# Query loads four slots sooner, and a new order of the last pair's products, in a fused attention and MLP kernel

## The chip, the cores and the metric

The kernel runs on one core of one Trainium2 chip. The metric is the device time of one execution in microseconds (us). Six runs of the kernel before have a median of 292.06 us (291.69 to 293.18).

## The reference

There are 8 batches of 8 heads, 576 positions and 64 features, in float32. Each batch goes through a linear attention with a cosine weighting, and its result through a two-layer network with a squared ReLU:

```python
q_p, k_p = phi(q), phi(k)      # phi(x) = [relu(x)*cos, relu(x)*sin], 128 features
kv  = einsum('bhsf,bhsd->bhfd', k_p, v);  z = sum(k_p, axis=2)
num = einsum('bhsf,bhfd->bhsd', q_p, kv)
den = einsum('bhsf,bhf->bhs', q_p, z)[..., None] + 1e-06
x   = (num / den) laid out as 4608 tokens x 512
h   = x @ w_in                 # 512 -> 2048
out = (relu(h) ** 2) @ w_out   # 2048 -> 512
```

## The kernel before

**Tiles and stages.** A batch is 576 tokens: four blocks of 128 (the "main" part) and a tail of 64. The tails of two neighbouring batches are handled together. `gemm1` makes h for 256 tokens (or for a double tail) in slices, ScalarE applies the ReLU into `rt`, VectorE squares it into `gT`. `gemm2` multiplies `gT` with `w_out`; from batch 1 on it does so for pairs of 128-token blocks with a seven-product scheme of the Strassen kind (`pair_mm`). A pair has two row blocks and two column halves of 256, so four result blocks `y[:, row, half]`. Seven products of eight 128x128x256 matmuls each (`product`, L523) go into four accumulators: `ya` and `yc` from the PSUM pool with the tag "yps", `yv` and `yu` from the pool with the tag "hps", which the h tiles of `gemm1` also use. VectorE forms sums of the left operand (`g_sum`, tiles `gs`, called S(1) to S(4)) and combines the products with `add` (L537). ScalarE copies two products out (`s1` at L561, `s5` at L576).

**The order of the work.** Nothing is scheduled automatically. A list of 144 slots holds one slice of `gemm1` or `gemm2` each; for every batch its `gemm1` slots start at `first[b]` and its `gemm2` slots at `second[b]`. For batches 2 to 7 `first` is 34, 50, 72, 88, 106, 122, and `second` is 42, 60, 80, 98, 114, 132. `at(slot, function, ...)` hangs further work behind a slot, `late` hangs the `g_sum` calls there, and `run` emits slot after slot. Each engine then works off its own instructions strictly in that order; engines wait for one another by semaphores alone. Attention work of a later batch is thus woven between the matmuls of an earlier one.

**Around the moved load.** For batches 4 to 7 the loop at L686 plans the attention of batch b while `gemm2` of batch b-2 runs. With o = second[b-2]: keys and values are turned into features from slot o on (`att_k`, `att_v`), `att_kv` multiplies them at o+3 and o+4, and the query features `att_feat` follow at o+4 to o+6: `feat_cos` on VectorE (L171), `feat_sin` on ScalarE (L181). The finished features are transposed by DMAs issued on the SP queue (L267). The loads are also issued on the SP queue: k and v (L688), then q at first[b-2]+9 (L689), one large transfer of 1 MB (L64) and two tails of 64 KB (L69) per tensor. The input pool holds two buffers of each tensor. The attention of batch b itself, and the transposes of its result x into `xT` and `xTt` (`att_x`, L342, on SP too), follow in `gemm1` of batch b-1; for batch 3 they stand at slots 39, 41 and 43, written out by hand (L678 to L685).

**The last pair.** For (batch 7, pair 1) `pair_mm` has an order of its own (L588 to L598): products p1 and p4, p5 and p6, p7 and p3, p2 in its four slots. The two row blocks leave in three transfers (`put`, L410): row 3 whole after p7, the right half of row 2 after p3, both on SP, and the left half of row 2 after p2, on ScalarE's queue.

Of the kernel before, what the change touches and what calls it, by code (L numbers as in the profile page):

```python
# [9 lines left out]
ALU = mybir.AluOpType  # L10
# [9 lines left out]
def kernel(  # L20
# [9 lines left out]
    nc = tc.nc  # L30
    P = nc.NUM_PARTITIONS
    B, H, S, D = q.shape
    F = 2 * D
    E1 = D + 1
    DM, DFF = moe_w_in.shape
    T = B * S
# [365 lines left out]
    def put(b, tt, y, c0=0, c1=DM, eng=None, n=1):  # L402

        eng = eng or (nc.sync if b == B - 1 else nc.gpsimd)
        dst = bass.AP(
            tensor=out.tensor,
            offset=(b * S + tt) * DM + c0,
            ap=[[J * DM, P], [1, n * DM if n > 1 else c1 - c0]],
        )
        eng.dma_start(out=dst, in_=y.rearrange("p i c -> p (i c)") if n > 1 else y[:, c0:c1])  # L410

    def put_tails(m, y):
        for k in range(2):
            dst = bass.AP(
                tensor=out.tensor,
                offset=((2 * m + k) * S + MAIN) * DM,
                ap=[[DM, TAIL], [1, DM]],
            )
            nc.gpsimd.dma_start(out=dst, in_=y[k * TAIL : (k + 1) * TAIL, :])

    def gemm2(b, s):
        if b == 0:

            if s == 0:
                yh = ps_h.tile([P, 2, DM], F32, name="yh", tag="hps", bufs=2)
                ypss[b] = [yh[:, 0, :], yh[:, 1, :]]
                for i in range(2):
                    yps = ps_y.tile([P, DM], F32, name="yps", tag="yps", bufs=2)
                    ypss[b].append(yps[:, :])
            for hb in range(s * HB // 8, (s + 1) * HB // 8):  # L430
                for tt in range(J):
                    nc.tensor.matmul(  # L432
                        out=ypss[b][tt],
                        lhsT=gTs[b][:, hb, tt * P : (tt + 1) * P],
                        rhs=w2sb[:, hb, :],
                        start=(hb == 0),
                        stop=(hb == HB - 1),
                    )
            if s == 7:
                for i in range(2):  # L440
                    y = mlp.tile([P, 2, DM], F32, name="ysb", tag="ysb", bufs=2)
                    for tt in range(2):
                        nc.scalar.copy(out=y[:, tt, :], in_=ypss[b][2 * i + tt])
                    put(b, 2 * i, y[:, :, :], n=2)
            return
        if b == 1 and s < 4:
            tile_mm(b, s // 2, s % 2)
            return
        pair_mm(b, PAIRS[b][s // 4], s % 4)
# [31 lines left out]
    HB2, DM2 = HB // 2, DM // 2  # L481
# [3 lines left out]
    def w2_block(i, j):  # L485
        return w2sb[:, i * HB2 : (i + 1) * HB2, j * DM2 : (j + 1) * DM2]

    def g_block(b, pair, i, j):
        if pair == 2:
            return gTts[b // 4 * 2 + i][:, j * HB2 : (j + 1) * HB2, :]  # L490
        c0 = (2 * pair + i) * P
        return gTs[b][:, j * HB2 : (j + 1) * HB2, c0 : c0 + P]
# [30 lines left out]
    def product(acc, lhs, rhs):  # L523
        for hb in range(HB2):
            nc.tensor.matmul(  # L525
                out=acc,
                lhsT=lhs[:, hb, :],
                rhs=rhs[:, hb, :],
                start=(hb == 0),
                stop=(hb == HB2 - 1),  # L530
            )

    def part_sum(name, n=1):
        return mlp.tile([P, n, DM2], F32, name=name, tag=name, bufs=1)

    def add(out, in0, in1, op=ALU.add):
        nc.vector.tensor_tensor(out=out, in0=in0, in1=in1, op=op)  # L537
# [3 lines left out]
    def pair_mm(b, pair, s):  # L541
        S = lambda n: sums[b, pair, n]
        T = lambda n: sums["T", n]
        a = lambda i, j: g_block(b, pair, i, j)
        if s == 0:
            d = pairs[b, pair] = {}
            for n in "ac":
                d[n] = ps_y.tile([P, DM], F32, name=f"y{n}", tag="yps", bufs=2)[:, 0:DM2]
            for n in "vu":
                d[n] = ps_h.tile([P, 2, FP], F32, name=f"y{n}", tag="hps", bufs=2)[:, 0, 0:DM2]  # L550
            d["s1"] = part_sum("s1")[:, 0, :]
            d["s5"] = part_sum("s5")
            d["u23"] = part_sum("u23", 2)
            d["y"] = mlp.tile([P, 2, DM], F32, name="ysb", tag="ysb", bufs=2)
        d = pairs[b, pair]
        u2, u3 = d["u23"][:, 0, :], d["u23"][:, 1, :]
        y = d["y"].rearrange("p i (j c) -> p i j c", j=2)

        def p1():
            product(d["a"], a(0, 0), w2_block(0, 0))  # L560
            nc.scalar.copy(out=d["s1"], in_=d["a"])  # L561

        def p2():
            product(d["c"], a(0, 1), w2_block(1, 0))
            add(y[:, 0, 0, :], d["c"], d["s1"])

        def p3():
            product(d["u"], S(4), w2_block(1, 1))
            add(y[:, 0, 1, :], d["u"], y[:, 0, 1, :])

        def p4():
            product(d["v"], a(1, 1), T(4))

        def p5():
            product(d["u"], S(1), T(1))
            nc.scalar.copy(out=d["s5"][:, 0, :], in_=d["u"])  # L576

        def p6():
            product(d["a"], S(2), T(2))
            add(u2, d["a"], d["s1"])  # L580

        def p7():
            product(d["c"], S(3), T(3))
            add(u3, d["c"], u2)
            add(y[:, 1, 0, :], u3, d["v"], ALU.subtract)
            add(y[:, :, 1, :], d["u23"][:, :, :], d["s5"].to_broadcast([P, 2, DM2]))

        if (b, pair) == (B - 1, 1):  # L588

            for fn in ((p1, p4), (p5, p6), (p7, p3), (p2,))[s]:  # L590
                fn()
                if fn is p7:
                    put(b, 3, d["y"][:, 1])
                if fn is p3:
                    put(b, 2, d["y"][:, 0], DM2, DM)
                if fn is p2:
                    put(b, 2, d["y"][:, 0], 0, DM2, nc.scalar)
            return  # L598
        for fn in ((p1, p4), (p2, p5), (p6, p7), (p3,))[s]:
            fn()  # L600
        if s == 3 and pair < 2:
            put(b, 2 * pair, d["y"][:, :, :], n=2)
        elif s == 3:
            for i in range(2):
                put_tails(b // 4 * 2 + i, d["y"][:, i])

    slots, first, second = [], {}, {}
# [6 lines left out]
    def at(s, fn, *args):  # L614
        after.setdefault(s, []).append((fn, args))
# [9 lines left out]
    def plan(b, k, f, kv, d, t=(), x=(), act_cos=(1, 3), act_v=range(NS)):  # L625


        for j in range(NS):
            last = j == J or j % 2
            at(k[j], att_k, b, j, feat_cos_act if j in act_cos else feat_cos)  # L630
            at(k[j], att_v, b, j, nc.scalar if j in act_v else nc.vector)
            at(f[j], att_feat, b, j)
            if t:
                at(t[j], att_t, b, j)
            elif last:
                at(f[j], att_qT, b, j // 2)
            at(d[j], att_d, b, j)
            if x:
                at(x[j], att_x_pe, b, j, x[j] > 16)
            elif last:  # L640
                at(d[j], att_x, b, j // 2)
        for i in range(2):
            at(kv[i], att_kv, b, i)


    for j in (2, 3):
# [15 lines left out]
        d=(11, 13, 15, 17, 19),  # L662
# [11 lines left out]
        d=(27, 28, 29, 31, 33),  # L674
# [8 lines left out]
        d=(38, 39, 40, 41, 43),  # L683
        act_cos=(0, 1, 2),
    )  # L685
    for b in range(4, B):  # L686
        o, p = second[b - 2], first[b - 1]
        at(34 if b == 4 else second[b - 3] + 6, load_batch, b, nc.sync, "kv")  # L688
        at(first[b - 2] + 9, load_batch, b, nc.sync, "q")  # L689
        plan(  # L690
            b,
            k=(o, o, o + 1, o + 1, o + 2),
            f=(o + 4, o + 4, o + 5, o + 5, o + 6),
            kv=(o + 3, o + 4),
            d=[p + j for j in range(NS)],
        )
# [7 lines left out]
    for b in range(1, B):  # L704
        for i, pair in enumerate(PAIRS[b]):
            if (b, i) == (1, 0):
                continue
            for n in range(1, 5):
                s = second[b] + 4 * i - 2 + (0, 1, 1, 2)[n - 1] if i else first[b] + 3 + n
# [83 lines left out]
```

## Time and profile before

| | |
|---|---|
| median of six runs | 292.06 us |
| the profiled execution's own time | 291.99 us |
| its span | 290.1 us, 1.89 us less than its time |
| granted TensorE clock | 1.00 |
| VectorE busy | 201.6 us (69%) |
| ScalarE busy | 164.0 us (57%) |
| GpSimd busy | 39.1 us (13%) |
| read from memory, written | 36.70 MB, 9.44 MB |
| q load of 1 MB on SP, issue to landing | 5.7 us median of 5 |
| v load of 1 MB on SP, issue to landing | 8.1 us median of 5 |

All times in the profile are microseconds from the start of the span. A row of the timeline gives the start, the busy time, the engine (PE is TensorE's matmul, DVE is VectorE, ACT is ScalarE, POOL is GpSimd, SPq and ACTq are the DMA-issuing queues of SP and ACT), the line of the kernel, the operation, what it writes and reads with shapes, and how many instructions were merged into the row. Brackets at the end give idle time before the row and what ended it. Matmuls are pipelined, so their rows overlap: eight matmuls of 128x256 show as 1.04 us but follow one another every 0.87 us.

### The profile page before, as it was taken

The page shows a single profiled execution, that of the slowest core. Times are in us where ns is not written, and L with a number is a line of the kernel's source. Part 1 is how long each engine was busy: PE and PEld are TensorE (multiplying, and loading weights), DVE is VectorE, ACT ScalarE, POOL GpSimd, SP SyncE. Part 2 cuts the span into 40 slices and gives each one's busy share as a digit, 9 for nine tenths or more (in the row PEclk, how much of TensorE's full clock was granted, in tenths as well). Part 3 has the DMA queues.
Part 4 walks back from the last instruction along what each step waited for, and adds up shares of the span by engine and source line. Part 5 has one row for each costly group of instructions (what it writes and reads, how often), then busy time and mean ns, then how long its engine had stood idle before and what let it go on. Part 6 is the DMA issues. An engine that isn't in the chain of part 4 may idle for free.

```text
span 290.1 us, 7292 instructions
## 1 busy us (share of the span) xinstructions
PE 281.9 (97%) x3045; PEld 236.0 (81%) x3045; DVE 201.6 (69%) x451; ACT 164.0 (57%) x250; POOL 39.1 (13%) x67
## 2 busy tenths in 40 slices
PE   8999999999999999899999999999999999999994
PEld 3579855888678888698988888988988888889883
DVE  1467765597497499677598776977677877546584
ACT  3575653679759668555782349834695451265110
POOL 1562504750000000000002000000000000000011
PEclk9999999999999999999999999999999999999999
DMA  7999995999637999899519985399809420300024
GB/s 214 297 205 286 352 214 166 357 378 292 92 112 189 210 240 152 238 288 256 166 75 214 348 161 160 93 270 300 220 0 225 124 46 2 145 2 2 0 78 141
DMA packets 76642, 53.04 MB, mean 183 GB/s; under 512 B 52001, under 2 KB 71713, under 8 KB 76609
## 3 DMA queue, kind: packets, MB, share of 16 engines
q1 hardware_dynamic: 66816, 29.24, 43.4%
q0 software_dynamic: 9648, 23.20, 27.0%
q8 instruction: 24, 0.39, 0.5%
q10 hardware_dynamic: 144, 0.13, 0.1%
q14 instruction: 10, 0.07, 0.1%
HBM read 36.70 MB, written 9.44 MB: 159 GB/s over the span
## 4 chain that ended last, share of the span: by engine, by line
PE 76%; DMA 11%; DVE 4%; issue 3%; ACT 2%; SPq 2%; POOL 1%; DVEq 0%; ACTq 0%; POOLq 0%
PE hps L383 37%; PE ya L525 8%; DMA q<-in_q_dram 8%; PE yc L525 8%; PE yu L525 7%; PE yv L525 4%; PE num L310 3%; DMA out_dram<-ysb 2%; PE yps L456 2%; PE kz L241 2%; DVE ysb L537 1%; SPq L69 1%; DVE u L537 1%; PE tq L284 1%; PE yps L432 1%
## 5 line engine op out<-in xcount | busy, mean ns | idle before, releaser
L383 PEld LDWEIGHTS <-w1sb 128*128 128x128 bf16 x1312 | 112.9, 98 | 12.8 <-issue 2.1
L383 PE MATMUL hps<-xT,w1sb 128*128 128x256 bf16 (+1 forms) x1056 | 119.1, 269 | 0.8 <-DVE ysb L537 0.2
L391 ACT ACTIVATE rt<-hps 128x1024 bf16<-128x1024 f32 x72 | 73.6, 1023 | 65.3 <-PE hps L383 42.9
L398 DVE TENSOR_TENSOR gT<-rt 128x1024 bf16<-128x1024 bf16 x64 | 44.0, 687 | 21.1 <-ACT rt L391 21.0
L525 PEld LDWEIGHTS <-gs 128*128 128x128 bf16 x480 | 46.8, 98 | 6.7 <-issue 1.2
L525 PEld LDWEIGHTS <-gT 128*128 128x128 bf16 x312 | 29.8, 98 | 3.5
L410 POOL DMA_DIRECT2D out_dram<-ysb x14 | 7.6, 541 | 172.4 <-DVE ysb L537 146.4
L181 ACT ACTIVATE qp<-q,sin_col 128x512 bf16<-128x512 f32 x32 | 22.1, 722 | 4.0 <-DMA q<-in_q_dram 4.0
L181 ACT ACTIVATE kp<-k,sin_col 128x512 bf16<-128x512 f32 x32 | 22.4, 717 | 3.2 <-DMA k<-in_k_dram 3.2
L324 DVE TENSOR_TENSOR x<-num,rden 128x512 bf16<-128x512 f32 x32 | 22.1, 691 | 1.1
L320 DVE TENSOR_SCALAR den<-num 128x8 f32<-128x8 f32 (+1 forms) x40 | 6.5, 163 | 21.1 <-PE num L310 20.9
L521 DVE TENSOR_TENSOR gs<-gT 128x1024 bf16<-128x1024 bf16 x26 | 17.8, 683 | 0.0
L171 DVE TENSOR_SCALAR qp<-q,cos_col 128x512 bf16<-128x512 f32 x32 | 14.6, 483 | 3.5 <-DMA q<-in_q_dram 3.5
L525 PE MATMUL yc<-w2sb,gs 128*128 128x256 bf16 x120 | 15.5, 273 | 1.0 <-DVE ysb L537 1.0
L525 PE MATMUL ya<-w2t,gs 128*128 128x256 bf16 x120 | 15.6, 273 | 0.0
L525 PE MATMUL yu<-w2sb,gs 128*128 128x256 bf16 x120 | 15.6, 273 | 0.0
L525 PE MATMUL yu<-w2t,gs 128*128 128x256 bf16 x120 | 15.5, 272 | 0.0
L383 PE MATMUL hps<-xTt,w1sb 128*128 128x128 bf16 x256 | 15.1, 219 | 0.2 <-ACT rt L391 0.2
L200 ACT CAST vext<-v 128x512 bf16<-128x512 f32 x23 | 14.1, 614 | 1.6 <-DMA v<-in_v_dram 1.6
L576 ACT COPY s<-yu 128x256 f32<-128x256 f32 x15 | 5.6, 372 | 15.7 <-PE yu L525 15.7
L525 PE MATMUL yc<-w2sb,gT 128*128 128x256 bf16 x104 | 13.5, 273 | 0.0
L525 PE MATMUL yv<-w2t,gT 128*128 128x256 bf16 x104 | 13.5, 273 | 0.0
(93 smaller groups left out, 333.7 us busy)
## 6 DMA issues: line engine op xcount, KB each, us to landing
out_dram<-ysb POOLq DMA_DIRECT2D x14, 512.0 KB, 4.3
k<-in_k_dram SPq DMA_DIRECT2D x5, 1024.0 KB, 7.1
v<-in_v_dram SPq DMA_DIRECT2D x5, 1024.0 KB, 8.1
q<-in_q_dram SPq DMA_DIRECT2D x5, 1024.0 KB, 5.7
q<-in_q_dram POOLq DMA_DIRECT2D x3, 1024.0 KB, 12.4
k<-in_k_dram POOLq DMA_DIRECT2D x3, 1024.0 KB, 9.1
v<-in_v_dram POOLq DMA_DIRECT2D x3, 1024.0 KB, 9.0
w1sb<-in_moe_w_in_dram POOLq DMA_DIRECT2D x4, 512.0 KB, 9.3
```

Source lines behind the costliest of these rows:

```text
L171: nc.vector.tensor_scalar(out=dst[:, :, 0:D], in0=src, scalar1=0.0, scalar2=cos_col[:, j : j + 1], op0=ALU.max, op1=ALU.mult,)
L181: nc.scalar.activation(out=dst[:, :, D:F], in_=src, func=ACTF.Relu, scale=sin_col[:, j : j + 1])
L200: copy(out=vx[:, j, h0:h1, 0:D], in_=piece("v", b, j)[:, h0:h1, :])
L310: nc.tensor.matmul(out=out, lhsT=lhsT, rhs=kvz[:, half * HH + hh, :], start=True, stop=True)
L320: nc.vector.tensor_single_scalar(out=den[:, 0:n], in_=n4[:, :, :, D], scalar=EPS, op=ALU.add)
L324: nc.vector.tensor_tensor(out=x_of(b, j).rearrange("p (b k) (l d) -> p b k l d", b=n, l=2), in0=n4[:, :, :, 0:D].rearrange("p b (k l) d -> ...
L383: nc.tensor.matmul(out=out, lhsT=w1sb[:, kb, hb * P : (hb + 1) * P], rhs=rhs, start=(kb == 0), stop=(kb == KB - 1),)
L391: nc.scalar.activation(out=rt[:, :, :], in_=hps[:, :, :], func=ACTF.Relu)
L398: nc.vector.tensor_tensor(out=dst, in0=rt[:, :, :], in1=rt[:, :, :], op=ALU.mult)
L410: eng.dma_start(out=dst, in_=y.rearrange("p i c -> p (i c)") if n > 1 else y[:, c0:c1])
L521: nc.vector.tensor_tensor(out=t[:, :, :], in0=in0, in1=in1, op=op)
L525: nc.tensor.matmul(out=acc, lhsT=lhs[:, hb, :], rhs=rhs[:, hb, :], start=(hb == 0), stop=(hb == HB2 - 1),)
```

## The change

It has two parts. In the loop over batches 4 to 7, the q load hangs four slots sooner, behind slots 39, 55, 77 and 93 where it was behind 43, 59, 81 and 97. In the last pair the seven products run in another order: p1, p2; p4, p6; p7, p5; and the product that was p3, now into accumulator `ya`. The product p5 is no longer copied out by ScalarE but added from PSUM by VectorE to the running sums; the one add over both rows becomes two adds of one row each. Each of the four result blocks leaves in a transfer of its own as soon as it is complete, three on SP and one on ScalarE's queue.

```diff
         if (b, pair) == (B - 1, 1):
 
-            for fn in ((p1, p4), (p5, p6), (p7, p3), (p2,))[s]:
-                fn()
-                if fn is p7:
-                    put(b, 3, d["y"][:, 1])
-                if fn is p3:
-                    put(b, 2, d["y"][:, 0], DM2, DM)
-                if fn is p2:
-                    put(b, 2, d["y"][:, 0], 0, DM2, nc.scalar)
+            if s == 0:
+                p1()
+                p2()
+                put(b, 2, d["y"][:, 0], 0, DM2)
+            elif s == 1:
+                p4()
+                p6()
+            elif s == 2:
+                product(d["c"], S(3), T(3))
+                add(u3, d["c"], u2)
+                add(y[:, 1, 0, :], u3, d["v"], ALU.subtract)
+                put(b, 3, d["y"][:, 1], 0, DM2)
+                product(d["u"], S(1), T(1))
+                add(u2, d["u"], u2)
+                add(y[:, 1, 1, :], d["u"], u3)
+                put(b, 3, d["y"][:, 1], DM2, DM, nc.scalar)
+            else:
+                product(d["a"], S(4), w2_block(1, 1))
+                add(y[:, 0, 1, :], d["a"], u2)
+                put(b, 2, d["y"][:, 0], DM2, DM)
             return
...
-        at(first[b - 2] + 9, load_batch, b, nc.sync, "q")
+        at(first[b - 2] + 5, load_batch, b, nc.sync, "q")
```

## The prediction

> **What bounds the kernel now.** I read the page's busy row first, then the list of waits, then the timeline around the one large TensorE wait and around the same stage of a later batch, then SP's own rows, and last the end of the span. From the page and from the waits (engine, line, what it waited for: total us, times, longest):
>
> ```profile
> PE 281.9 (97%) x3045; PEld 236.0 (81%) x3045; DVE 201.6 (69%) x451; ACT 164.0 (57%) x250; POOL 39.1 (13%) x67
> ```
>
> ```profile
> ACT qp L181 <- DMA q<-in_q_dram: 4.0, 2, 3.3
> ...
> PE yc L525 <- DVE ysb L537: 1.0, 1, 1.0
> ```
>
> TensorE is busy for 281.9 of 290.1 us at full clock. Of the 8.2 us it idles, 4.1 lie behind its last matmul (285.96 to 290.1), some 2 in the first 37 us, and the largest single wait between is the 1.0 us of `yc` for VectorE. The timeline shows what is behind it (batch 2's second pair, with batch 4's query features woven in):
>
> ```profile
> 117.15 1.04 PE L525 MATMUL ya<-w2t,gs 128*128 128x256 bf16 x8
> 117.95 1.33 ACT L181 ACTIVATE qp<-q,sin_col 128x512 bf16<-128x512 f32 x2 [3.29 <-DMA q<-in_q_dram]
> 117.95 0.88 DVE L171 TENSOR_SCALAR qp<-q,cos_col 128x512 bf16<-128x512 f32 x2 [1.80 <-DMA q<-in_q_dram]
> 118.75 0.41 DVE L537 TENSOR_TENSOR ysb<-yc,s 128x256 f32<-128x256 f32 x1
> 119.22 1.03 PE L525 MATMUL yc<-w2sb,gs 128*128 128x256 bf16 x8 [1.03 <-DVE ysb L537]
> ...
> 121.32 1.91 PE L383 MATMUL hps<-xT,w1sb 128*128 128x256 bf16 x16 [0.20 <-DVE ysb L537]
> ```
>
> VectorE idles 1.80 us, up to 117.95, for batch 4's q. The add that empties `yc` is queued behind those features in the in-order engine, so p7 can't write `yc` before 119.22, and the next `gemm1` starts at 121.32. The same stage for batch 6, where q landed long before (issued at 172.55), shows the same work without the wait:
>
> ```profile
> 185.45 0.87 DVE L171 TENSOR_SCALAR qp<-q,cos_col 128x512 bf16<-128x512 f32 x2
> ...
> 186.24 0.41 DVE L537 TENSOR_TENSOR ysb<-yc,s 128x256 f32<-128x256 f32 x1
> ...
> 186.52 1.04 PE L525 MATMUL ya<-w2t,gs 128*128 128x256 bf16 x8
> ...
> 187.40 1.04 PE L525 MATMUL yc<-w2sb,gs 128*128 128x256 bf16 x8
> ```
>
> Here `yc` follows `ya` after 0.88 us, and `hps` starts at 189.41, 2.89 us after `ya`. In batch 4's stage that stretch is 121.32 - 117.15 = 4.17 us. The stall is worth 4.17 - 2.89 = **1.28 us**, which is 1.03 + 0.20 and 0.05 of small change.
>
> **Part one, the q load.** In the emitted order SP's queue changes for batch 4 alone: q's three DMAs move from behind three transposes of batch 3's x (xT, xT, xTt) to behind the first of them. For batches 5, 6 and 7 no SP instruction lies between the old and the new place, so their SP order is the same; cost and gain nothing, and nothing there waits for q anyway. SP's rows, the second line from a view cut closer, so that it shows the first transpose alone:
>
> ```profile
> 100.57 3.78 SPq L69 DMA_DIRECT2D vt<-in_v_dram  x2
> 104.44 2.68 SPq L342 DMA_TRANSPOSE xT<-x  x1
> ...
> 110.68 1.17 SPq L342 DMA_TRANSPOSE xTt<-xt  x1
> 111.91 0.57 SPq L64 DMA_DIRECT2D q<-in_q_dram  x1
> ```
>
> SP is free of the first transpose at 104.44 + 2.68 = 107.12. The q buffer (batch 2's) and q's semaphores are long free, so q issues at about 107.2 instead of 111.91: 4.7 us sooner. It landed 6.02 us after issue before (in the chain of waits), which gives 113.2. Bounds: the fastest q load of the trace took 5.5 us, and the v load, of equal size and queued behind k, 8.2 us; so 112.7 to 115.4. ScalarE is ready for q at 114.66, VectorE at 116.15 (both ended their previous work there and idled). At 113.2 nobody waits. At 115.4 ScalarE starts its two sine rows 0.74 us late and ends them at 116.75; its next item that TensorE needs, the copy of `yu`, can't start before `yu` ends at 117.32. So over the whole bound the stall goes, and what is late next is the normal chain of the twin stage. I take -1.28 us.
>
> What the move puts behind q: q's issues take 0.57 + 1.29 us on SP, up to about 109.1, so the second xT, ready at 107.80 (x written) and issued up to 109.26 before, issues 109.1 to some 110.6. xTt needs xt, written at 110.65, and keeps its place. A rule of the Trainium skill speaks against the move: DMA: Bandwidth & Descriptors, section Queues, rings and completion order, says that one issuing queue's descriptors are taken in ring order on each engine. By it the second xT waits for the whole of q, so it lands after 113.2, at worst after 115.4 plus the 3.1 to 7.6 us that an xT transpose took in these rows: 123.0. By the rows alone it is 109.1 + 7.6 = 116.7. The first matmul on that half is the fifth slice of batch 3's `gemm1`, at 129.48 before and 128.2 after. Both leave over 5 us; cost nothing. If that cover were gone, TensorE would wait by the excess, one to one. The same rule protects v, which is ahead of q in the ring.
>
> Everything after 121.32 shifts as a block: among TensorE's waits none past that point is above 0.2 us, and the loads of batch 5 hang behind SP's transposes of batch 4, which come earlier too.
>
> **Part two, the last pair.** The same 56 matmuls, one ScalarE copy fewer (0.37 us, beside other work), one VectorE add more (one of 0.68 over two rows becomes two of 0.42), one DMA more. Before:
>
> ```profile
> 282.50 0.68 DVE L521 TENSOR_TENSOR gs<-gT,gs 128x1024 bf16<-128x1024 bf16 x1
> ...
> 284.92 1.04 PE L525 MATMUL yc<-w2sb,gT 128*128 128x256 bf16 x8
> 285.05 0.68 DVE L537 TENSOR_TENSOR ysb<-u,s 128x512 f32<-128x512 f32 x1
> 285.83 0.42 DVE L537 TENSOR_TENSOR ysb<-yu,ysb 128x256 f32<-128x256 f32 x1
> 286.17 0.41 DVE L537 TENSOR_TENSOR ysb<-yc,s 128x256 f32<-128x256 f32 x1
> 286.62 0.37 ACTq L410 DMA_DIRECT2D out_dram<-ysb  x1
> ```
>
> The last product ends at 284.92 + 1.04 = 285.96, but its add starts at 286.17, behind the two adds before it. After, by the 0.87 us step from 279.63: p1 279.63, p2 280.50, p4 281.37, p6 282.25, p7 283.12, p5 283.99, the last 284.87, ending at 285.91. The new wait is p7's on the add of y[0,0], since p2 now uses `yc` before it: on VectorE that add comes after the third `gs` (281.89 in the trace) at 282.50, ends at 282.92, and S(4) behind it moves to 282.84, ready by 283.52 for 284.87. Margin for p7: 0.2 us; each 0.1 us beyond costs 0.1. The further adds, 0.46 us apart where they depend on each other: u3 284.20, y[1,0] 284.66, u2 285.07, y[1,1] 285.53, and y[0,1] at 285.95, ending at 286.37. The last issue is at 286.41 on SP instead of 286.62 on ACT. A 128 KB store from SP took 2.5 us to land, one from ACT 2.4 (list of DMA issues): 288.91 against 289.02, **-0.11 us**. Here too a rule speaks against: the same page, section Bandwidth, wants transfers batched to 1 MiB, since each carries a fixed 2.0 us (measured there for GpSimd's queue); by its formula 256 KB cost 2.6 us and two halves 4.6 in sum. In this trace 256 KB took 2.5 and 128 KB 2.5, side by side, so only the last one's landing counts. Bounds: -0.4 (the final piece finds the queues emptier than before), +1.0 (it takes the 3.6 us of GpSimd's 128 KB stores). I take the nearest row, SP's.
>
> **Sum.** -1.28 - 0.11 = -1.39. The profiled execution goes from 291.99 to 290.60 (span 290.1 to 288.7). The median is 0.07 above it: 292.06 - 1.39 = 290.67, say 290.7.
>
> **Rivals.**
> - *Only part of q's wait goes.* SP's issue of q drags, as vt's two did (3.78 us at 100.57, for 64 KB each), and q lands at 116.7, midway between my upper bound and the old 117.93. VectorE then waits 0.55 of the 1.28: 291.2. Against it: q's large DMA is first in line, its tails can drag without harm. Chance 0.12.
> - *The gain is given back.* Some transfer or wait tied to another event takes the place of the stall, and the time stays at 292.0. For it: VectorE's slack is short. Against it: the twin stage runs without a wait behind it, and no large wait follows 121.32. Chance 0.12.
> - *The tail loses.* The last 128 KB lands like GpSimd's, 1.1 us later: 292.06 - 1.28 + 1.0 = 291.8. Chance 0.07.
> - *Slower: q takes v's bandwidth.* ScalarE already waits 0.24 us for v, which lands at 108.2, one us after q's new issue. Its casts then run without a gap to 114.40, and `att_kv`'s last products need the last cast at 114.58: 0.18 us of slack. A v that lands d late costs d - 0.2, so the change loses from d = 1.6 us. If q's 1.1 MB goes wholly ahead at the 360 GB/s that the timeline's windows show for loads, d = 3.1: 290.7 + 2.9 = 293.6. Against it: v is issued 7 us before q on the same queue, and q's first bytes came about a us after its issue. Chance 0.05.
>
> **How the numbers follow.** The forecast has 0.64, at 290.7 (290.2 to 291.1). The range of 289.9 to 291.8 holds it, the partial case and most of the lost tail, and a tail at its good bound; it leaves out the slower case and most of the given-back gain. A measurement of this kernel can tell about 0.3%, 0.88 us, from no change: faster means under 291.18. That is the forecast and two thirds of the partial case, 0.72; within is the rest, 0.23; slower 0.05.
>
> **What would show it.** Right: SP's q issue near 107.2; no wait of ACT or DVE on q; `yc` 0.88 us after `ya` there, `hps` near 120.0; the second xT later but no wait at `gemm1`'s fifth slice. At the end the last product near 284.87 - 1.28 and its add at once, no wait of p7 on VectorE. Wrong: v's cast waits over 0.24 us, q lands after 116.2, or the distance from the last add to the end of the span (3.5 us before) grows.

## The result, and the profile after

The changed kernel takes 289.93 us (median of 18 runs, 289.0 to 292.05) against 292.23 us of the kernel before in the same comparisons (39 runs). The ratio is 0.9921 with a 95% interval of 0.9904 to 0.9938: 2.3 us less, where 1.39 were forecast. 289.93 lies 0.03 us inside the low end of the stated range (289.9 to 291.8), below the likeliest case's own 290.2. The profiled executions of e2, e3 and e7 below (294.4, 295.2 and 294.4 us) are slower than their kernels' medians; from them only who waits for whom, distances of single steps and, for e3, the granted clock are used.

The stage of batch 4 after, from the timeline (start, busy time, engine, line, what it writes and reads):

```profile
113.90 1.33 ACT L181 ACTIVATE qp<-q,sin_col 128x512 bf16<-128x512 f32 x2
...
115.76 0.88 DVE L171 TENSOR_SCALAR qp<-q,cos_col 128x512 bf16<-128x512 f32 x2
...
116.84 1.04 PE L525 MATMUL ya<-w2t,gs 128*128 128x256 bf16 x8
...
117.71 1.04 PE L525 MATMUL yc<-w2sb,gs 128*128 128x256 bf16 x8
...
119.71 1.91 PE L383 MATMUL hps<-xT,w1sb 128*128 128x256 bf16 x16
```

In this stage no engine waits for q any more. `yc` follows `ya` after 0.87 us, and `hps` after 2.87 us where it took 4.17: 1.30 us less, as the twin stage of batch 6 said (1.28). SP's own rows show the new order:

```profile
103.04 2.70 SPq L342 DMA_TRANSPOSE xT<-x  x1
105.79 0.57 SPq L64 DMA_DIRECT2D q<-in_q_dram  x1
...
107.89 3.07 SPq L342 DMA_TRANSPOSE xT<-x  x1
111.05 1.20 SPq L342 DMA_TRANSPOSE xTt<-xt  x1
```

q issues at 105.79 and lands 6.55 us later, at 112.35, 1.5 us before ScalarE takes it up. SP came to it 1.4 us sooner than forecast (107.2), since its issues for v's tails took 2.12 us here and 3.78 before; in e1, the same order of loads, q issued at 107.43. The last pair after:

```profile
280.69 0.41 DVE L537 TENSOR_TENSOR ysb<-yc,s 128x256 f32<-128x256 f32 x1
...
281.32 1.04 PE L525 MATMUL yc<-w2sb,gs 128*128 128x256 bf16 x8
...
283.06 1.04 PE L525 MATMUL ya<-w2sb,gs 128*128 128x256 bf16 x8
...
284.05 0.37 ACTq L410 DMA_DIRECT2D out_dram<-ysb  x1
284.14 0.42 DVE L537 TENSOR_TENSOR ysb<-ya,u 128x256 f32<-128x256 f32 x1
```

The first add leaves `yc` at 281.10, 0.22 us before p7 takes it, so the new wait costs nothing. The last add starts 1.08 us after the last product started, where that took 1.25 before.

Where did 2.6 us of span (290.1 to 287.5) go? I follow marks that both timelines have:

| stretch | before | after | difference |
|---|---|---|---|
| start to batch 2's `hps` slice in the 95th us | 95.20 | 94.89 | -0.31 |
| from there to batch 3's first `hps` | 26.12 | 24.82 | -1.30 |
| from there to its second slice | 2.19 | 1.99 | -0.20 |
| from there to the last pair's p1 | 156.12 | 156.12 | 0.00 |
| p1 to the end of the last add | 6.95 | 6.74 | -0.21 |
| end of the last add to the end of the span | 3.52 | 2.94 | -0.58 |

Up to the mark of the first line both kernels emit the same instructions, so that line is scatter (95.60 in e1, 97.55 in e2 at the same mark). Without it the sum is -2.29, close to the difference of the medians. Spans are printed to 0.1 us, so the last line, and every stretch to the end below, is known to some 0.05 us. Forecast were -1.28 for the stall and, at the end, -0.21 for an earlier add and +0.10 for a longer landing; not forecast were the -0.20 and the -0.58.

The 0.20 us stands in the timeline of before, in a row that I had not charged. First before, then after:

```profile
123.25 0.30 PEld L310 LDWEIGHTS <-qpT 128*128 128x128 bf16 x8 [0.30 <-DMA qpT<-qp]
123.25 0.42 PE L310 MATMUL num<-kvz,qpT 128*128 128x65 bf16 x8
123.51 1.91 PE L383 MATMUL hps<-xT,w1sb 128*128 128x256 bf16 x16
```

```profile
121.35 0.39 PEld L310 LDWEIGHTS <-qpT 128*128 128x128 bf16 x8
121.46 0.41 PE L310 MATMUL num<-kvz,qpT 128*128 128x65 bf16 x8
121.70 1.91 PE L383 MATMUL hps<-xT,w1sb 128*128 128x256 bf16 x16
```

The late q also made its transposed features late, and the next attention product waited for them. The matmul row before that product is modelled to 123.23, so no idle time shows on PE; only the distance of the two `hps` slices, 2.19 against 1.99 us, tells of the loss.

The 0.58 us are the stores: the last one landed 2.40 us after its issue before and 1.84 us after it now, 0.56 us less. From the lists of DMA issues (size, median us from issue to landing), before and after:

```profile
out_dram<-ysb SPq DMA_DIRECT2D x1, 256.0 KB, 2.5
out_dram<-ysb SPq DMA_DIRECT2D x1, 128.0 KB, 2.5
out_dram<-ysb ACTq DMA_DIRECT2D x1, 128.0 KB, 2.4
```

```profile
out_dram<-ysb SPq DMA_DIRECT2D x3, 128.0 KB, 2.0
out_dram<-ysb ACTq DMA_DIRECT2D x1, 128.0 KB, 1.9
```

The 2.0 is the median of three: 3.6 us for the first, issued at 281.13 beside four tail stores of GpSimd, then 2.0 and, for the very last, 1.8. So 128 KB from SP have no one time to landing.

### The profile page after: what moved, and what is told of

Read it like the earlier page. It is cut to its first block, busy times and chain, and to the rows that moved or that the text cites. A ratio compares the mean times of both kernels' runs of the same rounds, so it can differ in the third digit from the quotient of the medians.

```text
span 287.5 us, 7293 instructions
## 1 busy us (share of the span) xinstructions
PE 281.5 (98%) x3045; PEld 236.2 (82%) x3045; DVE 201.7 (70%) x452; ACT 163.4 (57%) x249; POOL 39.1 (14%) x67
## 4 chain that ended last, share of the span: by engine, by line
PE 85%; DMA 5%; DVE 2%; ACT 2%; issue 2%; POOL 2%; ACTq 0%; DVEq 0%; POOLq 0%
PE hps L383 38%; PE ya L525 9%; PE yc L525 9%; PE yu L525 7%; PE yv L525 5%; PE wm L206 4%; PE kz L241 3%; PE num L310 3%; DMA v<-in_v_dram 3%; PE yps L456 2%; DMA out_dram<-ysb 2%; PE yps L432 1%; PE yh L432 1%; PE tq L284 1%; DVE ysb L537 1%
## 5 line engine op out<-in xcount | busy, mean ns | idle before, releaser
L525 PE MATMUL yu<-w2sb,gs 128*128 128x256 bf16 x112 | 14.5, 273 | 0.0
```

Of the source, the lines that this page charges most:

```text
L525: nc.tensor.matmul(out=acc, lhsT=lhs[:, hb, :], rhs=rhs[:, hb, :], start=(hb == 0), stop=(hb == HB2 - 1),)
```

## The experiments

The theory after the result: the two parts add, -1.5 us for the load (1.30 + 0.20) and -0.8 us for the last pair (0.21 + 0.58). Its rivals: the shorter end is scatter; the gain depends on how early q is issued; and, for the end, several readings of what makes a store land soon.

**e1, the load alone.**

```diff
-        at(first[b - 2] + 9, load_batch, b, nc.sync, "q")
+        at(first[b - 2] + 5, load_batch, b, nc.sync, "q")
```

> The earlier q load alone, with the old last pair. Theory (the parts add): the stall in batch 4's stage goes, 1.30 us, and with it 0.20 us that the first attention product after it waited for the query transposes, which are late when q is; ratio to before 0.995, -1.5 us, and the stretch from the last add to the end of the span stays near 3.5 us. Rival (the whole difference of the two kernels comes from the load, and the shorter end is scatter of the landing): -2.1 to -2.3 us.

Measured: 290.87 us, ratio 0.9943 (0.9922 to 0.9965), -1.7 us. In its profile the stretch from the last add to the end is 3.51 us, and the second slice follows the first after 1.98 us (120.44 to 122.42). The theory holds; the rival's -2.1 lies inside the interval of the time, but the stretch of 3.51 us speaks against it.

**e2, the last pair alone.** The changed kernel with the q load back at `+ 9`.

> The new last pair alone, with q loaded where it was. Theory: -0.8 us, of which 0.2 is the earlier last add and 0.6 the shorter stretch from that add to the end (2.9 us in place of 3.5); the wait of yc in batch 4's stage stays at 1.0 us. Rival (the shorter end was scatter): -0.1 to -0.2 us and a stretch near 3.5 us.

Measured: 291.49 us, ratio 0.9964 (0.9953 to 0.9975), -1.1 us. The stretch is 2.88 us (289.62 to 292.5). So the shorter end is no scatter: it is 3.51, 3.51 and 3.56 us in e1, e3 and e4, all with the old pair. The sum of e1 and e2 is -2.8 us; with their intervals it agrees with the -2.3 of both parts together. In this profiled execution q was issued at 114.78 and landed at 121.24, and `yc` waited longer than in the kernel before:

```profile
122.53 1.03 PE L525 MATMUL yc<-w2sb,gs 128*128 128x256 bf16 x8 [2.00 <-DVE ysb L537]
```

The expectation of 1.0 us for that wait missed. Counted from the same `hps` slice (97.55 here, 95.20 before), q was issued 0.5 us later and took 0.4 us longer to land, and the wait grew by the sum. With the load at its old place the stall thus varies; in none of the nine profiles with an earlier load behind k and v (changed, e1, e4 to e10) does `yc` wait.

**e3, q ahead of k and v.** Batch 4's q is loaded with k and v at slot 34, in the order q, k, v; the old pair.

```diff
-        at(34 if b == 4 else second[b - 3] + 6, load_batch, b, nc.sync, "kv")
-        at(first[b - 2] + 9, load_batch, b, nc.sync, "q")
+        at(34 if b == 4 else second[b - 3] + 6, load_batch, b, nc.sync, "qkv" if b == 4 else "kv")
+        if b > 4:
+            at(first[b - 2] + 9, load_batch, b, nc.sync, "q")
```

> Batch 4's q is loaded sooner still, ahead of its k and v on the same queue; old last pair. Theory of the slower rival (what v loses TensorE loses, beyond 0.2 us of slack): v lands about 3.1 us later (1.1 MB at 360 GB/s), ScalarE's casts start that much later, TensorE loses 2.9 us less the 1.5 us that q no longer costs: +1.4 us, with ACT waiting for v in place of q. Rival (the engines share out the transfers, or v has more room than 0.2 us): like the load moved alone, -1.5 us.

Measured: 294.13 us, ratio 1.0062 (1.0038 to 1.0086), +1.8 us. SP's issue of v before, then the timeline of e3:

```profile
99.92 0.55 SPq L64 DMA_DIRECT2D v<-in_v_dram  x1
```

```profile
104.74 0.55 SPq L64 DMA_DIRECT2D v<-in_v_dram  x1
...
111.94 0.62 ACT L200 CAST vext<-v 128x512 bf16<-128x512 f32 x1 [2.66 <-DMA v<-in_v_dram]
...
114.20 0.36 ACT L576 COPY s<-yu 128x256 f32<-128x256 f32 x1
...
114.61 1.03 PE L525 MATMUL yu<-w2sb,gs 128*128 128x256 bf16 x8 [2.50 <-ACT s L576]
...
116.07 1.90 PE L525 MATMUL ya<-w2sb,gT 128*128 128x256 bf16 x8
...
117.76 1.78 PE L525 MATMUL yv<-w2t,gT 128*128 128x256 bf16 x8
```

The sign is that of the forecast's slower case, but the cause is another. v lands at 111.91 where it landed at 108.15, because SP issues it 4.8 us later, behind q and k; from issue to landing it takes 7.2 us, and took 8.2 before. So this run doesn't show q taking bandwidth from v. ScalarE's casts wait for v, and behind two of them in its in-order queue stands the copy of `yu`. TensorE's next product into `yu` waits for that copy, before it reaches `att_kv`, which I had named: it starts 3.54 us after the product ahead of it where the step is 0.87, so 2.67 us are lost. That is v's delay of 3.8 us, less the 0.5 us by which TensorE's own work is later in this execution, less the 0.66 us that the copy had to spare before (it ended at 110.81, the product came at 111.47).

A second loss follows that neither expectation has. From 115.9 to 119.3 us, shortly after that wait, the granted clock is 0.50, and the products `ya` and `yv` take 3.31 us from their start to the next row's where they took 1.75 before: 1.6 us more. Three of e3's seven executions have a mean clock of 0.992 to 0.994, as 3.4 us at half clock give, and take 294.7 to 295.2 us. The other four, at 0.997 or more, have a median of 293.7: 1.1 us above the kernel before (292.6 in this comparison), near the 2.7 lost less the 1.5 that a late q no longer costs. After the wait of 2.00 us in e2's profile the clock stayed at 1.00.

**e4, two slots sooner instead of four.** `first[b - 2] + 7`, which puts q behind the second xT transpose; the old pair.

> The q load two slots sooner instead of four, so behind the second xT transpose and ahead of the tail's; old last pair. Theory (q has about 3 us of room, since VectorE needs it only at 116): q issues near 109.3, lands near 115.3, and the gain is the whole 1.5 us. Rival (the gain grows with how early q is issued, because the queue behind it also counts): about half, -0.7 us.

Measured: 290.85 us, ratio 0.994 (0.992 to 0.9959), -1.8 us: the whole gain. q issued at 110.35 and landed 6.5 us later, at 116.88, later than I had expected; VectorE waited for it:

```profile
116.90 0.89 DVE L171 TENSOR_SCALAR qp<-q,cos_col 128x512 bf16<-128x512 f32 x2 [0.31 <-DMA q<-in_q_dram]
```

Still `yc` follows `ya` after 0.87 us (117.59 to 118.46). This bounds the room for `p7`: VectorE needs 0.8 us for two feature rows and 0.41 for the add before p7 at 118.46, so for it q may land up to about 117.2 in this profile. For the transposed features there is hardly any room left: they land at 122.13, the first weights from them are loaded 1.70 us after `hps` starts where it is 1.63 in e1, and the product itself starts after 1.75 (1.74 in e1).

**e5, e6 and e7, what makes the stores land sooner.** e5 is the changed kernel with row 3 leaving whole, 256 KB on ScalarE's queue after its second half. e6 is e1 with row 3 in halves. e7 is the changed kernel with row 2 leaving whole at the end.

```diff
 # e5
-                put(b, 3, d["y"][:, 1], 0, DM2)
-                put(b, 3, d["y"][:, 1], DM2, DM, nc.scalar)
+                put(b, 3, d["y"][:, 1], 0, DM, nc.scalar)
 # e6, in the old order of products
-                    put(b, 3, d["y"][:, 1])
+                    put(b, 3, d["y"][:, 1], 0, DM2)
+                    put(b, 3, d["y"][:, 1], DM2, DM, nc.scalar)
 # e7
-                put(b, 2, d["y"][:, 0], 0, DM2)
-                put(b, 2, d["y"][:, 0], DM2, DM)
+                put(b, 2, d["y"][:, 0])
```

> Both parts of the change, but row 3 leaves whole (256 KB on ScalarE's queue when its second half is added) where it left in halves. The order of the products and the last store (128 KB on SP) are those of the changed kernel. Theory (the last store lands sooner because less data is queued in the last microsecond): the stretch from the last add to the end goes from 2.9 us back towards 3.5, about 3.3, and the time is 0.4 us above the changed kernel's: -1.9 us to before. Rival (the order of the products or the spacing of the stores does it): 2.9 us stays, -2.3 us.

> The earlier q load with the old order of products, but row 3 leaves in two halves, one on each queue, right after the add that completes it. Theory (data queued in the last microsecond): 384 KB still leave within 0.9 us of the last issue, so the stretch stays near 3.4 us and the time near that of the load moved alone, -1.6 us. Rival (smaller pieces land sooner as such): 2.9 us, -2.1 us.

> Both parts of the change, but row 2 leaves whole at the very end, 256 KB on SP, where its left half left 3.5 us sooner. Theory (data queued at the end): 384 KB leave in the last 0.6 us, the stretch goes to 3.3 us or more, -1.9 us to before. Rival (only the number of stores or the order of products counts): 2.9 us, -2.3 us.

The packets in the traces split the time to landing of the last store: from its issue to its first data packet, its data packets themselves, and from the last of these to the landing.

| kernel | last stores, in order of issue | last one, us to landing | split of it | last add to end, us | ratio to before |
|---|---|---|---|---|---|
| before | 256, 128, 128 KB in 0.9 us | 2.40 | 1.05, 0.55, 0.80 | 3.52 | 1 |
| changed | 128, 128 KB in 0.5 us | 1.84 | 0.85, 0.52, 0.47 | 2.94 | 0.9921 (0.9904 to 0.9938) |
| e5 | 256, 128 KB in 0.5 us | 2.13 | 1.00, 0.54, 0.59 | 3.23 | 0.9935 (0.9915 to 0.9955) |
| e6 | four of 128 KB in 1.5 us | 2.09 | 0.88, 0.53, 0.68 | 3.20 | 0.9936 (0.9918 to 0.9955) |
| e7 | 128, 256 KB in 0.5 us | 2.32 | 0.84, 0.83, 0.65 | 3.43 | 0.9932 (0.991 to 0.9954) |

The packets of the last store before (ScalarE's queue, 287.66 to 288.23 us) and after (SP's, 285.43 to 285.97), all 128 KB of it in 128 packets and 16 small ones (queue: packets, MB, share of 16 engines):

```profile
q10 hardware_dynamic: 144, 0.13, 69.8%
```

```profile
q1 hardware_dynamic: 144, 0.13, 72.1%
```

The times of the last four differ by less than their intervals; the landings and stretches decide. One profile each is enough for that, since the landing repeats: 2.40, 2.40 and 2.38 us in e1, e3 and e4 with the old pair, 1.85 in e2 with the new one. e5 and e7 come out as the theory said (3.3, and 3.3 or more), with the product order and the last add untouched: one store of 256 KB among the last two brings back 0.29 or 0.48 of the 0.56 us. That is not all of it. e6 has no store of 256 KB and lies between both of its expectations (3.4 and 2.9); its four pieces leave over 1.5 us where three left in 0.9, the last two of them 0.33 us apart (0.54 in the changed kernel), so it doesn't separate the size of the pieces from how much leaves shortly before the last. What is shown is that the last store lands later with 256 KB in it or just ahead of it. Waiting behind other packets is the smaller part of that: of the 0.56 us, 0.20 lie before the first packet and 0.33 behind the last one, where no packet of the store is left to move.

**e8, e9 and e10, the last block in smaller pieces.** The last 128 KB leave as two 64 KB stores: in e8 as two halves of 64 partitions on SP and ScalarE's queue at once, in e9 as two halves of the columns with all 128 partitions on the same two queues, in e10 like e8 but both on SP.

```diff
 # e8 (e10 has nc.sync twice)
-                put(b, 2, d["y"][:, 0], DM2, DM)
+                for p0, eng in ((0, nc.sync), (64, nc.scalar)):
+                    dst = bass.AP(tensor=out.tensor,
+                        offset=(b * 576 + 2) * DM + DM2 + p0 * J * DM,
+                        ap=[[J * DM, 64], [1, DM2]])
+                    eng.dma_start(out=dst, in_=d["y"][p0 : p0 + 64, 0, DM2:DM])
 # e9
-                put(b, 2, d["y"][:, 0], DM2, DM)
+                put(b, 2, d["y"][:, 0], DM2, DM2 + P)
+                put(b, 2, d["y"][:, 0], DM2 + P, DM, nc.scalar)
```

> Both parts of the change, and the last 128 KB leave as two halves of 64 partitions at once, one on each queue: tried as a faster version. Theory (what is left of the stretch is fixed cost of a store and the end of the program): no gain, 2.9 us stays, -2.3 us to before. Rival (size of the last piece still counts): 2.7 us, -2.5 us.

> Both parts of the change, the last block again as two stores at once on the two queues, but cut by columns, so that each has 128 partitions (512 B per row). One look. Theory A (two queues that issue at the same moment hold each other up): each issue takes 0.5 us or more and the last lands after 2.3 us or more, as with the halves by partitions. Theory B (stores of 64 partitions are slow as such): 0.35 us per issue, 1.8 us to landing, stretch 2.9 us.

> Both parts of the change, the last block as two halves of 64 partitions one after the other on SP. One look. Theory A (simultaneous issue): 0.33 us per issue, the second issue 0.33 us later, each lands after 1.8 us, stretch 3.2 us. Theory B (64 partitions): each issue 0.5 us and landing 2.3 us, stretch near 3.9 us.

Measured: e8 took 290.38 us, ratio 0.9933 (0.9915 to 0.9951), with a stretch of 3.46 us and landings of 2.3 and 2.4 us, so both of its expectations failed. e9 and e10 were run once each: stretches of 2.92 and 3.83 us, issues and landings near those of theory B. Their stores, first e9 (all of SP's and of ScalarE's at the end), then e10 (ns least, median, most per issue):

```profile
L410 SPq DMA_DIRECT2D out_dram<-ysb x4: 332/344/382, 273.5 to 284.6; - x4
...
L410 ACTq DMA_DIRECT2D out_dram<-ysb x2: 366/370/374, 284.1 to 284.6; - x2
```

```profile
L615 SPq DMA_DIRECT2D out_dram<-ysb x2: 557/570/583, 285.9 to 286.5; - x2
```

A store of 64 partitions took 0.54 us or more to issue and 2.1 us or more to land, on two queues at once (e8) or one after the other on SP (e10), and its data moved 1.2 us or more after its issue; one of 128 partitions and the same 64 KB took 0.33 to 0.37 us to issue and landed after 1.7 to 1.9. The rows of 1 KB are not the reason, since the changed kernel's 128 KB stores have them too and issue in 0.33 to 0.37 us. Two queues issuing at once made no issue longer in e9. And 64 KB in place of 128 KB gained nothing: e9's stretch is the changed kernel's. No version tried here beats the changed kernel beyond its interval.

## Why the prediction was right, and where it was short

The stall was understood and sized; that the time still lies in the range, by 0.03 us, is close to luck. 0.9 of the 2.3 us come from what the forecast did not have: 0.20 for the transposed features, and 0.68 for the stretch behind the last add, which it took to be 0.10 longer and which came out 0.58 shorter.

- **The stall of batch 4.** Right in place, mechanism and size: 1.30 us against 1.28. The twin stage of batch 6 gave the size better than the idle time of the `yc` row alone (1.03).
- **What the move puts behind q.** Right: the second xT transpose issued at 107.89 and landed 5.8 us later, at 113.7, 1.4 us behind q and sooner than both figures of the forecast (116.7 and 123.0), and no matmul waited for it. The section that the forecast cites there (Trainium skill, DMA: Bandwidth & Descriptors, section Queues, rings and completion order) gives the order in which descriptors are taken and says that completion is not in that order, so a landing behind the whole of q was more than it states. v was not delayed; its first cast on ScalarE doesn't wait in the profile after.
- **Everything after shifts as a block, with nothing more to gain there.** Short by 0.20 us: the wait for `qpT` at 123.25 was part of the same lateness. I had listed TensorE's idle times, and this one is hidden by the modelled end of the row ahead of it. The twin stage had it: its second slice starts 1.98 us after its first (189.41 to 191.39), so the same comparison carried one mark further would have given 0.2 us. e1 shows the loss gone (1.98 us).
- **The order of the last pair.** Right: the last add ends 0.21 us sooner after p1, as worked out, and p7 waits for nothing.
- **The last store.** The mis-sized term. I took the 2.5 us of SP's 128 KB store as a property of that store and forecast -0.11 for the whole end. That store had left 0.5 us behind one of 256 KB; the changed kernel's last one, 0.5 us behind one of 128 KB, took 1.8 us, and the end gained 0.21 + 0.58 = 0.79. My lower bound of -0.4 named the very case (queues emptier than before) and was too narrow. The formula that the forecast takes from the same page (Trainium skill, DMA: Bandwidth & Descriptors, section Anatomy of one DMA, for GpSimd's queue) gives an estimate of 0.3 us between 256 and 128 KB. e7's last store took 0.48 us longer than the changed kernel's, 0.31 of it in its own packets.
- **The rivals.** Partial gain: no. Its sum charged VectorE's wait one to one, but 0.31 us of it cost `p7` nothing in e4, and 1.80 us cost 1.03 before. Given back: no, 156.12 us on both sides. Lost tail: the opposite. Slower: e3 is slower because v is issued later; that q takes v's bandwidth is not shown by any run. Its slack of 0.18 us was a misreading too: the products at 114.58 read `vext`, whose last cast ended at 113.69, and those that read the last cast's `vextt` start at 115.16. The tightest place was the copy of `yu`, with 0.66 us.

What stays open: why the time from a store's last packet to its landing varies from 0.47 to 0.80 us, so also why e6's last store took 2.09 us with 128 KB pieces only. The number of stores under way at once and their bytes were not told apart. Nor is it known what set off the low clock in three of e3's executions.

## What to carry to other kernels

To price a stall, compare the stage with a later one that does the same work without it, and measure distances between starts of the same matmuls: idle time on TensorE's row misses losses that hide under modelled ends (0.20 us here). Where a load is late, follow its consumers one step further (its features, their transposes, the product that reads them). At the end of a kernel, try last stores that are small and have little just ahead of them, with all 128 partitions in each. The time to landing of one store is no constant: here 128 KB took from 1.8 to 2.5 us among the last stores alone, depending on what left shortly before.

## What the runs showed of the hardware that I had not expected

- A store of 64 partitions and 64 KB issued in 0.54 to 0.58 us and landed after 2.1 to 2.4; one of 128 partitions and 64 KB issued in 0.33 to 0.37 us and landed after 1.7 to 1.9 (e8, e10 against e9).
- Halving the last store from 128 to 64 KB with 128 partitions left the stretch at 2.92 us (2.94 with 128 KB), while doubling it to 256 KB made it 3.43 (e7).
- The part behind the last landing was about 1.1 us in both kernels: 289.02 to 290.1 before, 286.4 to 287.5 after.
- From the last data packet of the last store to its landing it took 0.80 us before and 0.47 us in the changed kernel, more of the difference than the wait for the first packet (1.05 and 0.85 us after the issue).
- In three of e3's seven executions the mean clock was 0.992 to 0.994. The profiled one had the granted clock at 0.50 for 3.4 us, beginning 1.25 us after TensorE's wait of 2.50 us had ended.
